# Second feed-forward layer in units of 512 tokens instead of 384, with four output accumulators

## Chip, cores and metric

One core of one Trainium2 chip. The metric is the device time of one execution in microseconds (us), median over several runs. The engines are TensorE (PE: matmuls, and PEld: its weight loads), VectorE (DVE), ScalarE (ACT), GpSimd (POOL) and SyncE (SP, which issues DMAs).

## What is computed

```python
y = linear_attention(q, k, v, alpha)              # batch 4, heads 8, 768 tokens, 48 channels
x = y.transpose(0, 2, 1, 3).reshape(3072, 384)
h = x @ w_in1                                     # 384 -> 2048
g = where(h >= 1, h, where(h <= -1, 0, (h + 1) ** 2 / 4))
x = g @ w_out1                                    # 2048 -> 384
h = x @ w_in2                                     # 384 -> 2048
out = (h * cos(h)) @ w_out2                       # 2048 -> 384
```

The weights come as float64; everything else is float32.

## The kernel before

The 3072 tokens are cut into NU = 8 units of N = 384. Attention comes first, chunk by chunk; the first layer runs beside it and after it, then the second layer. The 2048 hidden channels of a layer are FT = 16 hidden tiles of 128.

**Order of the program.** Every operation is handed to a list scheduler (`Order.add`) with its engine, a rough length, the operations it comes after and the ring buffers it takes (`buf(tag)`). The scheduler simulates the engines with these rough lengths and writes the instructions in the order in which they start there. Each engine then runs its own instructions strictly in that order on the chip. What a hidden tile of a unit needs is a *step*.

**Products.** A product of two float32 matrices is done as three matmuls on parts hi and lo (`mm3`): hi·hi + hi·lo + lo·hi. A step of the second layer (`step2(i)`, i = 16·unit + hidden tile) has 9 *input products* (`ff_in`: 3 blocks of model channels × 3 passes, 384 moving columns, the tokens, into one PSUM bank of h, h, sc, y by turns) and 9 *output products* (`ff_out`: 3 blocks of 128 tokens × 3 passes, 384 moving columns, the model channels, onto three accumulators). The accumulators of a unit are three of acc0, acc1, acc2, kv, one further with each unit; each collects 16 steps.

**Between input and output products** a step passes through a chain: ACT scales h into an angle (L1044), DVE rounds it to whole turns (`nearest`, L1048), subtracts (`rest`, L1051), ACT takes the sine (L1054), DVE multiplies by h (`product`, L1057), ACT rounds that to gh (L896), POOL computes gl = g − gh (L901). In PE's order the output products of step i stand behind the input products of step i + 2.

**Weights of the second layer.** Each of the 32 weight tiles (16 of w_in2, 16 of w_out2) needs two conversions of half a tile each, thus 64, on DVE: a shift (L343), a select of sign and exponent (L347) and a merge with the low word (L353), the last from a stage in `w_raw` or in the attention's buffers `am`; ACT and POOL make hi and lo of it (L364, L368). They are spread over the end of the first layer and the first steps of the second. The first layer's steps have two DVE instructions each (L947, L951).

**Once per unit** the inputs are split into x2s (ACT L1023, POOL L1027, three each), and the finished accumulators are copied out (`put`, two on ACT, one on DVE) and stored.

Of the kernel before, what the change touches and what calls it, by code (L numbers as in the profile page):

```python
# [45 lines left out]
class Buf:  # L46
    """A buffer of a ring: its first user takes a slot, its last one gives it back."""
# [16 lines left out]
class Order:  # L64
    """List scheduling: the operations of the program, each with its engine, a rough length in us,
    the operations it comes after and the buffers it takes, put into the order of emission."""
# [24 lines left out]
    def run(self):  # L91
# [10 lines left out]
        def since(op):  # L102
            """When op can start, or None."""
# [50 lines left out]
def gla_two_mlps(  # L154
# [60 lines left out]
    rings.update({f"{t}_2": 1 for t in SECOND})  # L215
    o = Order(rings, loose=("kv", "acc0", "acc1", "h"))
# [5 lines left out]
    # rough lengths in us  # L222
# [17 lines left out]
    # constants  # L240
# [7 lines left out]
    # buffers whose padding is written once  # L248
    am_b = [one.tile([P, 2, N], F32, name=f"am{i}") for i in range(2)]
    v_b = [one.tile([P, CH, 112], F32, name=f"v{i}") for i in range(NV)]  # L250
    raw_b = [one.tile([P, R * D], F32, name=f"raw{i}") for i in range(NRAW)]
# [29 lines left out]
    def weight(layer, kind, f, after=()):  # L281
        """One hidden tile; of the first layer's input weights, two come in one load."""
# [15 lines left out]
        if joint:  # L298
            pair_of["buf"] = rb

# [89 lines left out]
    SQUARES = []  # L390
    xraw = []
# [6 lines left out]
    def early_buffers():  # L398
        """The first unit's alpha, k and q have room where later units' x1 come."""
# [23 lines left out]
    def attention(m):  # L423
# [8 lines left out]
        def room(pool_, tag):  # L432
            if alt and tag in SECOND:
                return xraw[2][1][0][:, SECOND.index(tag), :]
            return pool_.tile([P, N], F32, tag=tag, name=tag)

        # loads
        loads, rawb = [], []
        for x, src in enumerate((alpha, k, q)):
# [31 lines left out]
            rawb.append(rb)  # L471
        if early:
            vb, v_ops = v0b, v0_ops
        else:
            vb = buf("v")

# [14 lines left out]
        # channel-major alpha, k, q; the running products F, then 1/F from the chunk's end  # L491
        ab, kb, qb, fb, gb, feb, amb = (
            buf(t + "_2" if alt and t in SECOND else t) for t in ("ta", "tk", "tq", "F", "G", "fe", "am")
        )
        if alt:
# [3 lines left out]
        def turn(x, pool_, tag, tb):  # L499
            def fn():  # L500
                d[tag] = room(pool_, tag)
# [17 lines left out]
        def evict(bank, tag, pool_, tb, after):  # L519
            def fn():  # L520
                d[tag] = room(pool_, tag)
# [4 lines left out]
        if turned:  # L526
            a_src, k_src, q_src = (buf("h") for _ in range(3))
            ta, tk, tq = (turn_by_pe(x, bank) for x, bank in enumerate((a_src, k_src, q_src)))
            if not k_direct:
                tk = evict(k_src, "tk", p2, kb, tk)  # L530
            if not q_direct:
                tq = evict(q_src, "tq", p2, qb, tq)
        else:
            a_src = ab
            ta, tk = turn(0, p1, "ta", ab), turn(1, p2, "tk", kb)
# [4 lines left out]
        def forward():  # L540
            d["F"] = room(p1, "F")
# [23 lines left out]
        if not turned:  # L565
            tq = turn(2, p2, "tq", qb)

        def last():
            d["G"] = room(p1, "G")
# [17 lines left out]
        def times(tag, src, by, direct, pool_, tb, by_buf, after):  # L587
            """k/F and q*F, from PSUM or in place."""
            def fn():
                if direct:  # L590
                    d[tag] = room(pool_, tag)
# [10 lines left out]
        ksc = times("tk", k_src if turned else kb, "G", k_direct, p2, kb, gb, [bw, tk])  # L602
        qs = times("tq", q_src if turned else qb, "F", q_direct, p2, qb, fb, [fw, tq])

        def square(i, nm):
            def fn():
                if turned and i == 0:
                    d["ta"] = room(p1, "ta")
# [13 lines left out]
        # k/F with the tokens on the partitions  # L622
# [39 lines left out]
        # products within the chunks: both heads at once, on the two halves of the array's rows  # L662
# [33 lines left out]
        # the state: what each chunk adds, then chunk by chunk  # L696
# [19 lines left out]
        def within_and_before(cs):  # L716
            """Outputs of the chunks cs: tokens of the same chunk, then the state before it."""
# [71 lines left out]
        # hi and lo parts; channels of the last two heads fill the gaps of the others' tiles  # L789
# [79 lines left out]
    def ff_in(layer, f, x, x_ops, xbuf, tag):  # L869
# [3 lines left out]
        def fn():  # L873
            h.tile = ps(tag)
            for j in range(KT):
                xt = x()
                mm3(
                    h.tile[:, 0:N],
# [7 lines left out]
            "pe", 3 * KT * pe(N), fn, [w_op, *x_ops, prev.get("in")], new=[h], use=[hb, lb, xbuf], span=6 * KT * pe(N) + STEP  # L886
# [4 lines left out]
    def split_g(g, rb, after, final=False):  # L891
        ghb, glb = buf("gh"), buf("gl")

        def high():
            ghb.tile = p3.tile([P, N], F32R, tag="gh", name="gh")
            nc.scalar.copy(ghb.tile, g())  # L896

        def low():
            glb.tile = p3.tile([P, N], F32R, tag="gl", name="gl")
# [3 lines left out]
        a = add("act", act(N, 0.04), high, [after], new=[ghb], use=[rb])  # L903
        a = add("dve" if final else "pool", dve(N) if final else pool(N), low, [a], new=[glb], use=[rb, ghb])
        return a, ghb, glb

    def ff_out(layer, f, acc, first, last, g):
# [3 lines left out]
        for c in range(KT):  # L911
# [25 lines left out]
    def step1(u, f, first, last, add_):  # L937
        h_op, h = ff_in(1, f, lambda: X1[u]["x"], X1OPS[u], X1B[u][0], "h")
        rb = buf("r")

        def relu():
            rb.tile = p3.tile([P, N], F32, tag="r", name="r")
# [10 lines left out]
        def below():  # L953
            rb.tile = p3.tile([P, N], F32, tag="r", name="r")
# [8 lines left out]
        if u < len(ACT_STEPS) and f in ACT_STEPS[u]:  # L963
            # min(r, 1) = 1 - relu(1 - r), and its square against h
# [48 lines left out]
    X2S = {}  # L1013

    def split_x2(u, after):
        t = {}
        xb = buf("x")
        ops = []
        for c in range(KT):
            def high(c=c):  # L1020
                if c == 0:
                    t["x"] = xp.tile([P, KT, 2, N], F32R, tag="x", name="x2s")
                nc.scalar.copy(t["x"][:, c, 0, :], X2[u // 2]["x"][:, u % 2, c, :])  # L1023

            def low(c=c):
                hi, lo = t["x"][:, c, 0, :], t["x"][:, c, 1, :]
                nc.gpsimd.tensor_tensor(out=lo, in0=X2[u // 2]["x"][:, u % 2, c, :], in1=hi, op=ALU.subtract)  # L1027
# [295 lines left out]
```

## Time and profile before

| | |
|---|---|
| median of 3 runs | 1039.32 us (1036.25 to 1042.29) |
| span of the profiled execution | 1041.0 us |
| PE busy | 976.2 us, 94% |
| DVE busy | 737.8 us, 71% |
| ACT, POOL busy | 487.1 us, 442.7 us |

The profiled execution is 1.7 us above the median. The second layer takes the stretch from about 602 us, when the first layer's last step leaves DVE, to 1033 us; its weights are still being converted until about 652 us. In the trace's views, a timeline row is "start in us, duration in us, engine, line, operation, output<-input, shapes, count", then in brackets how long the engine had been idle and what released it. A row of a group is "line, engine, operation, names, shapes, count | busy us, mean ns of one | idle time of the engine just before them, and by what it ended". A row of a window is "from:to, length, busy us (and count) of PE, PEld, DVE, ACT and POOL, granted clock of PE, DMA share, GB/s". Matmuls are pipelined, so one lasts longer than the distance from its start to the next one's; that distance is what it costs.

### The profile page before, as it was taken

The numbers are of one execution on the slowest core, as the hardware profiler recorded it, in microseconds if no ns is written. First come the engines' busy times: TensorE is split into PE (matmuls) and PEld (weight loads), VectorE is DVE, ScalarE is ACT, GpSimd is POOL, SyncE is SP. The second block draws the span as 40 slices with busy tenths as digits, with TensorE's granted clock in tenths as the row PEclk, the third lists the DMA queues.
The fourth block names the chain that finished last, engine by engine and source line by source line (L and its number), as shares of the span: only waits on it lengthen the run. The fifth ranks groups of instructions, "written<-read, shape, count | busy, mean of one in ns | idle before, by whom it ended". The sixth has DMA issues, their size and how long they took to land.

```text
span 1041.0 us, 17456 instructions
## 1 busy us (share of the span) xinstructions
PE 976.2 (94%) x6186; PEld 894.3 (86%) x6186; DVE 737.8 (71%) x1370; ACT 487.1 (47%) x1108; POOL 442.7 (43%) x458
## 2 busy tenths in 40 slices
PE   7998878999999999999999878999999999999996
PEld 6677867788888889889899777899999999999996
DVE  6899999876778767674448999656565656565653
ACT  4566555443333434433345565545454545454443
POOL 3266665443333333332246566434343434343332
PEclk9899999999999999999999989999999999999999
DMA  7968753443534334330203421000000000000000
GB/s 167 181 148 168 159 151 87 110 113 72 114 86 110 76 79 102 66 70 8 82 30 102 126 91 61 24 1 23 1 21 4 23 1 24 1 23 1 25 1 26
DMA packets 113553, 71.82 MB, mean 69 GB/s; under 512 B 71729, under 2 KB 96305, under 8 KB 113457
## 3 DMA queue, kind: packets, MB, share of 16 engines
q1 hardware_dynamic: 113456, 70.62, 28.5%
q8 instruction: 50, 0.82, 0.3%
q14 instruction: 47, 0.38, 0.1%
HBM read 58.79 MB, written 9.44 MB: 66 GB/s over the span
## 4 chain that ended last, share of the span: by engine, by line
DVE 28%; PE 11%; ACT 10%; issue 7%; POOL 1%; DVEq 0%; POOLq 0%; ACTq 0%
DVE turn L1048 8%; DVE ang L1051 7%; DVE ang L1057 6%; ACT ang L1054 6%; PE acc L865 5%; PE h L865 4%; ACT ang L1044 3%; DVE wz L353 2%; DVE wz L347 2%; DVE wz L343 1%; DVE h L947 0%; POOL gl L901 0%; PE y L865 0%; DVE r L951 0%; PE y L725 0%
## 5 line engine op out<-in xcount | busy, mean ns | idle before, releaser
L901 POOL TENSOR_TENSOR gl<-ang,gh 128x384 fp32r<-128x384 f32 x127 | 136.3, 1073 | 241.3 <-ACT gh L896 215.7
L901 POOL TENSOR_TENSOR gl<-r,gh 128x384 fp32r<-128x384 f32 x128 | 135.5, 1059 | 191.0 <-ACT gh L896 159.6
L865 PE MATMUL h<-x,winhi 128*128 128x384 f32 x768 | 201.9, 344 | 13.2 <-DVE r L951 8.1
L865 PEld LDWEIGHTS h<-x,winhi 128*128 128x128 f32 x768 | 140.2, 191 | 18.1 <-DVE r L951 10.8
L1048 DVE TENSOR_SCALAR turn<-ang 128x384 int32<-128x384 f32 x128 | 95.1, 743 | 72.6 <-ACT ang L1044 72.6
L865 PE MATMUL acc<-gh,wouthi 128*128 128x384 f32 x384 | 136.2, 355 | 3.7 <-DVE x L997 1.5
L1054 ACT ACTIVATE ang<-ang 128x384 f32<-128x384 f32 x128 | 67.3, 526 | 151.5 <-DVE ang L1051 151.5
L865 PE MATMUL acc<-gl,wouthi 128*128 128x384 f32 x384 | 131.7, 343 | 5.9 <-POOL gl L901 5.9
L865 PE MATMUL h<-x,winlo 128*128 128x384 f32 x384 | 131.0, 341 | 0.0
L865 PE MATMUL acc<-gh,woutlo 128*128 128x384 f32 x384 | 129.7, 338 | 0.0
L947 DVE TENSOR_TENSOR h<-r,h 128x384 f32<-128x384 f32 x119 | 66.3, 557 | 82.8 <-ACT r L943 82.8
L896 ACT CAST gh<-r 128x384 fp32r<-128x384 f32 x128 | 65.5, 511 | 101.0 <-DVE r L951 96.8
L865 PE MATMUL acc<-wouthi,gl 128*128 128x384 f32 x288 | 101.3, 352 | 8.7 <-POOL gl L901 8.7
L865 PE MATMUL acc<-wouthi,gh 128*128 128x384 f32 x288 | 98.8, 343 | 7.0 <-ACT x L999 2.4
L943 ACT ACTIVATE r<-h,half 128x384 f32<-128x384 f32 x119 | 68.8, 578 | 77.6 <-PE h L865 77.5
L865 PE MATMUL h<-x2s,winhi 128*128 128x384 f32 x384 | 97.7, 335 | 1.7 <-DVE r L951 1.7
L865 PE MATMUL acc<-woutlo,gh 128*128 128x384 f32 x288 | 97.6, 339 | 0.0
L896 ACT CAST gh<-ang 128x384 fp32r<-128x384 f32 x128 | 65.6, 513 | 55.3 <-DVE ang L1057 55.2
L1051 DVE TENSOR_TENSOR ang<-ang,turn 128x384 f32<-128x384 f32 x128 | 81.9, 640 | 11.7
L865 PEld LDWEIGHTS acc<-gh,wouthi 128*128 128x128 f32 x384 | 72.4, 189 | 12.3 <-issue 2.8
L865 PEld LDWEIGHTS acc<-gl,wouthi 128*128 128x128 f32 x384 | 72.5, 189 | 10.6 <-POOL gl L901 10.3
L865 PEld LDWEIGHTS h<-x,winlo 128*128 128x128 f32 x384 | 73.0, 190 | 0.2 <-POOL winlo L368 0.2
(152 smaller groups left out, 2109.0 us busy)
## 6 DMA issues: line engine op xcount, KB each, us to landing
w_raw<-in_moe_w_out_dram SPq DMA_DIRECT2D x18, 384.0 KB, 3.6
scr<-G SPq DMA_DIRECT2D x96, 48.0 KB, 1.8
ks<-scr SPq DMA_DIRECT2D x24, 192.0 KB, 2.8
out_dram<-o SPq DMA_DIRECT2D x24, 192.0 KB, 2.0
v<-in_v_dram SPq DMA_DIRECT2D x56, 72.0 KB, 2.4
w_raw<-in_moe_w_in_dram SPq DMA_DIRECT2D x10, 384.0 KB, 3.2
raw<-in_alpha_dram SPq DMA_DIRECT2D x48, 72.0 KB, 2.0
raw<-in_k_dram SPq DMA_DIRECT2D x48, 72.0 KB, 2.0
```

Source lines behind the costliest of these rows:

```text
L347: nc.vector.scalar_tensor_tensor(out=z, in0=t["y"], scalar=-(2**31), in1=z, op0=ALU.bitwise_and, op1=ALU.bitwise_or)
L353: nc.vector.scalar_tensor_tensor(out=z, in0=bits(0).bitcast(U32), scalar=29, in1=z, op0=ALU.logical_shift_right, op1=ALU.bitwise_or,)
L865: nc.tensor.matmul(o, lhsT=lhs[a], rhs=rhs[b], start=first and i == 0, stop=last and i == 2)
L896: nc.scalar.copy(ghb.tile, g())
L901: eng.tensor_tensor(out=glb.tile, in0=g(), in1=ghb.tile, op=ALU.subtract)
L943: nc.scalar.activation(rb.tile, h.tile[:, 0:N], AF.Relu, bias=half, scale=0.5)
L947: nc.vector.tensor_tensor(out=hh, in0=rb.tile, in1=hh, op=ALU.max)
L1044: nc.scalar.activation(rb.tile, h.tile[:, 0:N], AF.Copy, bias=0.25, scale=1.0 / TWO_PI)
L1048: nc.vector.tensor_scalar(out=tb.tile, in0=rb.tile, scalar1=1.0, scalar2=None, op0=ALU.mult)
L1051: nc.vector.tensor_tensor(out=rb.tile, in0=rb.tile, in1=tb.tile, op=ALU.subtract)
L1054: nc.scalar.activation(rb.tile, rb.tile, AF.Sin, scale=SIN_SCALE)
L1057: nc.vector.tensor_tensor(out=rb.tile, in0=rb.tile, in1=h.tile[:, 0:N], op=ALU.mult)
```

## The change

The second layer's units become M = 512 tokens, NU2 = 6 of them instead of 8: 96 steps instead of 128. An input product has 512 moving columns instead of 384, and so has every instruction of the chain; a step has 12 output products instead of 9 (four blocks of 128 tokens, 384 columns each) onto all four accumulators, and a unit ends with four copies out (two on ACT, two on DVE). The number of moving columns in all is the same: 128 × 18 × 384 = 96 × (9 × 512 + 12 × 384) = 884,736; the matmuls of the layer are 2016 instead of 2304.

The larger buffers lie in rooms that the attention and the first layer have left: angles in the rooms of the first layer's r and gh (4 buffers), turns in that of gl (2), the second layer's gh and gl in two tiles of x1 (4 each), the units' x2s by turns in `rv` (the attention's raw and v) and `amt` (am, tk, tq), the copies out in those of F, G, ta and ks. `over(...)` makes the first user of a room wait for the last ones of the old buffers.

```diff
+    rings.update({"xs": 2, "ang": 4, "turn": 2, "gh2": 4, "gl2": 4, "o0": 1, "o1": 1, "o2": 1, "o3": 2})
...
-    am_b = [one.tile([P, 2, N], F32, name=f"am{i}") for i in range(2)]
...
+    amt = one.tile([P, 8, N], F32, tag="amt", name="amt")
+    am_b = [amt[:, 2 * i:2 * i + 2] for i in range(2)]
...
+    rv = one.tile([P, NRAW * R * D + NV * CH * 112], F32, tag="rv", name="rv")
...
+    M = 512
+    NU2 = NT // M
+    G2 = M // P
...
+    def second_buffers():
+        def take_angles():
+            F2["ang"] = [t_[:, i] for tag in ("r", "gh") for t_ in [p1.tile([P, 2, M], F32, tag=tag, name="ang")] for i in range(2)]
+            t_ = p1.tile([P, 2, M], I32, tag="gl", name="turn")
+            F2["turn"] = [t_[:, i] for i in range(2)]
+
+        F2["op"] = add(None, 0.0, take_angles, over("r", "g"), lat=0.0)
...
     def step2(i):
-        u, f = divmod(i, FT)
-        t, xb, x_ops = X2S[u]
-        h_op, h = ff_in(2, f, lambda: t["x"], x_ops, xb, H2TAGS[i % len(H2TAGS)])
-        rb, tb = buf("r"), buf("ks")
+        u2, f = divmod(i, FT)
+        t, xb, x_ops = X2S[u2]
+        h_op, h = ff_in(2, f, lambda: t["x"], x_ops, xb, H2TAGS[i % len(H2TAGS)], M)
+        rb, tb = buf("ang"), buf("turn")
...
         if f == 0:
-            step2.acc = [buf(ACC2TAGS[(u * KT + c) % 4]) for c in range(KT)]
+            step2.acc = [buf(tag) for tag in ACC2TAGS]
...
-        for c in range(KT):
-            tag, pool_ = (("tk", p2), ("tk", p2), ("tq", p2))[c]
-            ob = buf(tag)
+        for c in range(G2):
+            ob = buf(f"o{c}")
...
-                copy = nc.vector.tensor_copy if c == 1 else nc.scalar.copy
+                copy = nc.vector.tensor_copy if c % 2 else nc.scalar.copy
```

Up to about 530 us of the trace of before the program's order is the same on all engines. The first place where the order matters below is DVE where the first layer ends. Here L951 is the last of the first layer's products, L343, L347 and L353 are the three instructions of a conversion (wy and wz its work buffers), and L1048, L1051 and L1057 are turn, rest and product of the second layer's first step. Before:

```order
L951 SCALAR_TENSOR_TENSOR r<-r,h 128x384
L347 SCALAR_TENSOR_TENSOR wz<-wy,wz 128x384
L353 SCALAR_TENSOR_TENSOR wz<-am_94,wz 128x384
L1048 TENSOR_SCALAR turn<-ang 128x384
L343 TENSOR_SCALAR wz<-wy 128x384
L1051 TENSOR_TENSOR ang<-ang,turn 128x384
L347 SCALAR_TENSOR_TENSOR wz<-wy,wz 128x384
L353 SCALAR_TENSOR_TENSOR wz<-w_raw,wz 128x384
L1057 TENSOR_TENSOR ang<-ang,h 128x384
```

After (where L973 is the first layer's last product, L353, L357 and L363 the conversion, L1109, L1112 and L1118 turn, rest and product, and L1019 a copy of a finished accumulator of the first layer):

```order
L973 SCALAR_TENSOR_TENSOR r<-r,h 128x384
L353 TENSOR_SCALAR wz<-wy 128x384
L357 SCALAR_TENSOR_TENSOR wz<-wy,wz 128x384 x2
L363 SCALAR_TENSOR_TENSOR wz<-w_raw,wz 128x384 x2
L353 TENSOR_SCALAR wz<-wy 128x384
L357 SCALAR_TENSOR_TENSOR wz<-wy,wz 128x384
L1019 COPY x_6030<-acc_6071 128x384
L353 TENSOR_SCALAR wz<-wy 128x384
L363 SCALAR_TENSOR_TENSOR wz<-w_raw,wz 128x384
L1109 TENSOR_SCALAR turn<-ang 128x512
L357 SCALAR_TENSOR_TENSOR wz<-wy,wz 128x384
L1112 TENSOR_TENSOR ang<-ang,turn 128x512
```

The first layer's last product now stands ahead of more of the conversions: 47 of the 64 are ahead of it instead of 51, and 4 stand between it and the second layer's first product instead of 2.

The second place is DVE where the last of the 64 conversions ends. Before:

```order
L343 TENSOR_SCALAR wz<-wy 128x384
L1057 TENSOR_TENSOR ang<-ang,h 128x384
L347 SCALAR_TENSOR_TENSOR wz<-wy,wz 128x384
L1048 TENSOR_SCALAR turn<-ang 128x384
L353 SCALAR_TENSOR_TENSOR wz<-w_raw,wz 128x384
L1051 TENSOR_TENSOR ang<-ang,turn 128x384
L1048 TENSOR_SCALAR turn<-ang 128x384
L1051 TENSOR_TENSOR ang<-ang,turn 128x384
L1057 TENSOR_TENSOR ang<-ang,sc 128x384
```

After:

```order
L363 SCALAR_TENSOR_TENSOR wz<-w_raw,wz 128x384
L1112 TENSOR_TENSOR ang<-ang,turn 128x512
L353 TENSOR_SCALAR wz<-wy 128x384
L357 SCALAR_TENSOR_TENSOR wz<-wy,wz 128x384
L1118 TENSOR_TENSOR ang<-ang,y 128x512
L363 SCALAR_TENSOR_TENSOR wz<-w_raw,wz 128x384
L1109 TENSOR_SCALAR turn<-ang 128x512
L1112 TENSOR_TENSOR ang<-ang,turn 128x512
L1118 TENSOR_TENSOR ang<-ang,h 128x512
```

The last conversion stood behind the tenth of the second layer's products and now stands behind the twelfth.

## Rows read from the trace of the kernel before

**Rows 1.** The page: the span.

```profile
span 1041.0 us, 17456 instructions
```

**Rows 2.** Windows: end of layer 1, rest of conversion, and what follows.

```profile
556.00:602.00 46.00, 39.60 (x210) 35.66 (x209) 44.88 (x66) 26.20 (x55) 29.50 (x28) 1.00 0.42 129
602.00:656.00 54.00, 42.18 (x212) 38.09 (x210) 50.83 (x77) 31.49 (x67) 31.92 (x28) 0.94 0.21 66
660.00:1020.00 360.00, 356.52 (x2013) 349.00 (x2012) 215.54 (x344) 171.05 (x367) 137.84 (x130) 1.00 0.04 12
```

**Rows 3.** Groups on DVE from 556 to 655 us.

```profile
L347 DVE SCALAR_TENSOR_TENSOR wz<-wy,wz 128x384 int32<-128x384 int32 x27 | 26.1, 967 | 0.3
L353 DVE SCALAR_TENSOR_TENSOR wz<-w_raw,wz 128x384 uint32<-128x384 uint32 x17 | 17.1, 1016 | 0.2
L343 DVE TENSOR_SCALAR wz<-wy 128x384 int32<-128x384 int32 x27 | 14.5, 537 | 0.6 <-POOL woutlo L368 0.6
L353 DVE SCALAR_TENSOR_TENSOR wz<-am,wz 128x384 uint32<-128x384 uint32 x10 | 9.6, 960 | 0.1
L1051 DVE TENSOR_TENSOR ang<-ang,turn 128x384 f32<-128x384 f32 x12 | 9.5, 795 | 0.1
L1048 DVE TENSOR_SCALAR turn<-ang 128x384 int32<-128x384 f32 x12 | 7.7, 638 | 1.3 <-ACT ang L1044 1.3
...
L1057 DVE TENSOR_TENSOR ang<-ang,h 128x384 f32<-128x384 f32 x6 | 3.3, 542 | 0.0
```

**Rows 4.** Timeline of DVE: last first-layer product, two turns, twelfth second-layer product.

```profile
602.08 0.54 DVE L951 SCALAR_TENSOR_TENSOR r<-r,h 128x384 f32<-128x384 f32 x1
...
604.67 0.35 DVE L1048 TENSOR_SCALAR turn<-ang 128x384 int32<-128x384 f32 x1
...
610.27 1.16 DVE L1048 TENSOR_SCALAR turn<-ang 128x384 int32<-128x384 f32 x1
...
654.67 0.55 DVE L1057 TENSOR_TENSOR ang<-ang,y 128x384 f32<-128x384 f32 x1
```

**Rows 5.** Timeline of POOL, beside the second of these turns.

```profile
609.89 1.32 POOL L901 TENSOR_TENSOR gl<-ang,gh 128x384 fp32r<-128x384 f32 x1
```

**Rows 6.** Timeline of PE: outputs of the eleventh step of layer 2.

```profile
655.14 0.44 PE L865 MATMUL acc<-wouthi,gh 128*128 128x384 f32 x1 [0.70 <-ACT gh L896]
```

**Rows 7.** Timeline of PE: first input, first output, next first input product.

```profile
627.15 0.51 PE L865 MATMUL sc<-x2s,winhi 128*128 128x384 f32 x2
...
628.71 0.34 PE L865 MATMUL acc<-wouthi,gh 128*128 128x384 f32 x1
...
630.30 0.51 PE L865 MATMUL y<-x2s,winhi 128*128 128x384 f32 x2
```

**Rows 8.** Window: a short stretch of layer 2's first steps.

```profile
614.77:617.95 3.18, 3.18 (x11) 3.18 (x11) 3.15 (x6) 1.97 (x4) 2.03 (x2) 0.50 0.44 134
```

**Rows 9.** Timeline of PE within that stretch.

```profile
616.04 0.84 PE L865 MATMUL y<-x2s,winhi 128*128 128x384 f32 x2
...
617.00 0.84 PE L865 MATMUL y<-x2s,winhi 128*128 128x384 f32 x2
```

**Rows 10.** Timeline of PE in the attention: small products, weights of 128 columns.

```profile
31.34 0.45 PE L630 MATMUL acc<-ident,tk 112*128 112x112 f32 x3
31.63 0.45 PE L630 MATMUL kv<-ident,tk 112*128 112x112 f32 x3
```

**Rows 11.** Timeline of PE: waits of two unit changes, four units apart.

```profile
729.77 0.44 PE L865 MATMUL acc<-wouthi,gl 128*128 128x384 f32 x1 [0.63 <-POOL gl L901]
...
937.44 0.45 PE L865 MATMUL acc<-wouthi,gl 128*128 128x384 f32 x1 [0.63 <-POOL gl L901]
```

**Rows 12.** Timeline of PE: the end.

```profile
1026.80 0.34 PE L865 MATMUL acc<-wouthi,gh 128*128 128x384 f32 x1
...
1030.27 0.45 PE L865 MATMUL acc<-wouthi,gl 128*128 128x384 f32 x1 [0.64 <-POOL gl L901]
...
1033.02 0.34 PE L865 MATMUL kv<-wouthi,gl 128*128 128x384 f32 x1
```

More of the change, by code (lines that the diff above doesn't have):

```diff
@@ L299, in weight @@
             pair_of["buf"] = rb
+        if layer == 2 and i > 2:
+            ARENAS["amt"].append(rb)
         def place():
@@ L471, in attention @@
             rawb.append(rb)
+            if not in_x:
+                ARENAS["rv"].append(rb)
         if early:
@@ L585, in attention, with times @@
         bw = add("dve", CH * 0.26, backward, [la], use=[a_src, feb, gb])
[L587 removed]
+        def times(tag, src, by, direct, tb, by_buf, after):
             def fn():
                 if direct:
[L591 removed]
+                    d[tag] = room(tag, tb)
                 eng = nc.vector if direct else nc.gpsimd
@@ L910, in ff_out @@
         ops = []
-        for c in range(KT):
+        for c in range(len(acc)):
             def fn(c=c):
@@ L1011, in step1, with over, take @@
             X2OPS[u, c] = [p]
-    X2S = {}
-    def split_x2(u, after):
+    M = 512
+    NU2 = NT // M
+    G2 = M // P
+    X2S, GX, F2 = {}, [], {}
+    def over(*names):
+        return [x for name in names for b_ in ARENAS[name] for x in b_.ops()]
+    def second_buffers():
[4 more added lines that the diff above has]
+        F2["op"] = add(None, 0.0, take_angles, over("r", "g"), lat=0.0)
+        for _ in range(2):
+            xb, t_ = buf("x"), {}
+            def take(t_=t_):
+                t_[0] = xp.tile([P, 4, M], F32R, tag="x", name="g2")
+            add(None, 0.0, take, new=[xb], lat=0.0)
+            GX.append((xb, t_))
@@ L1016, in split_x2 @@
+    def split_x2(u2):
         t = {}
-        xb = buf("x")
+        xb = buf("xs")
         ops = []
-        for c in range(KT):
[L1020 to L1027, printed above, removed]
-            a = add("act", act(N, 0.04), high, X2OPS[u, c] + after, new=[xb] if c == 0 else [], use=[xb] if c else [])
-            ops.append(add("pool", pool(N), low, [a], use=[xb]))
@@ L1031, in split_x2, with take, src, high @@
-        X2S[u] = (t, xb, ops)
+        def take():
+            tag = ("rv", "amt")[u2 % 2]
+            t["x"] = one.tile([P, KT, 2, M], F32R, tag=tag, name="x2s")
+        first = add(None, 0.0, take, over(("rv", "amt")[u2]) if u2 < 2 else [], new=[xb], lat=0.0)
+        parts, s0 = [], u2 * M
+        while s0 < (u2 + 1) * M:
+            e0 = min((s0 // N + 1) * N, (u2 + 1) * M)
+            parts.append((s0 // N, s0 % N, e0 - s0, s0 - u2 * M))
+            s0 = e0
+        for c in range(KT):
+            for u, at, n, to in parts:
+                def src(c=c, u=u, at=at, n=n):
+                    return X2[u // 2]["x"][:, u % 2, c, at:at + n]
+                def high(c=c, n=n, to=to, src=src):
+                    nc.scalar.copy(t["x"][:, c, 0, to:to + n], src())
+                def low(c=c, n=n, to=to, src=src):
+                    nc.gpsimd.tensor_tensor(
+                        out=t["x"][:, c, 1, to:to + n], in0=src(), in1=t["x"][:, c, 0, to:to + n], op=ALU.subtract
+                    )
+                a = add("act", act(n, 0.04), high, [*X2OPS[u, c], first], use=[xb, X2B[u // 2]])
+                ops.append(add("pool", pool(n), low, [a], use=[xb, X2B[u // 2]]))
@@ L1056, in product @@
         def product():
[L1057 to L1064 removed]
+            nc.vector.tensor_tensor(out=rb.tile, in0=rb.tile, in1=h.tile, op=ALU.mult)
+        a = add("act", act(M), angle, [h_op, F2["op"]], new=[rb], use=[h])
+        a = add("dve", dve(M / 2), nearest, [a], new=[tb], use=[rb])
+        a = add("dve", dve(M), rest, [a], use=[rb, tb])
+        a = add("act", act(M, 0.04), sine, [a, RELU[-1]], use=[rb])
+        a = add("dve", dve(M), product, [a], use=[rb, h])
+        g = split_g(lambda: rb.tile, rb, a, layer=2, final=i == NU2 * FT - 1)
         if f == 0:
[L1066 removed]
+            step2.acc = [buf(tag) for tag in ACC2TAGS]
         acc = step2.acc
@@ L1127, in gla_two_mlps @@
         weight(2, "out", f, after=GLA_END[-1:])
-    for u in range(NU):
-        split_x2(u, [])
+    second_buffers()
+    for u2 in range(NU2):
+        split_x2(u2)
         for f in range(FT):
-            step2(u * FT + f)
+            step2(u2 * FT + f)
     with tc.manual_schedule():
```

97 lines of the change are left out of this document (54 added, 43 removed).

## The prediction, made before the changed kernel ran

> **What bounds the kernel now.** I read the windows first, since the page's mean over the span [rows 1] hides stages. The second layer falls in two. From 556 to 656 us DVE is busy 44.88 of 46 and 50.83 of 54 us, PE only 39.60 and 42.18: DVE, which converts the weights, sets the pace. From 660 to 1020 us PE is busy 356.52 of 360 us and DVE 215.54: PE sets it [rows 2]. So a change is worth what it does to DVE's work up to the last conversion, and behind that what it does to PE's products and waits.
>
> I mark the border at one event: DVE has done all 64 conversions and twelve products of the chain, at 655.22 us [rows 4]. At the same moment PE starts the outputs of the layer's eleventh step, at 655.14 us, after waiting 0.70 us for gh [rows 6]. By then it has done 13 steps' input and 10 steps' output products, so 115 and 118 are left.
>
> **Prices of before.** Nine input products take 628.71 − 627.15 = 1.56 us, nine output products 630.30 − 628.71 = 1.59 us [rows 7]: 173.5 and 176.7 ns each. At the 2.4 GHz of that stretch (granted clock 1.00 [rows 2]) 384 columns are 160 ns, so 13.5 and 16.7 ns stand over. What is left costs 115 × 1.56 + 118 × 1.59 = 367 us. PE ends at 1033.02 + 0.34 = 1033.4 us [rows 12], 378.2 us after 655.14; so 11 us go to waits. Seven of them are visible: once per unit PE waits for gl. The waits at 729.77 and 937.44 us [rows 11] are four units apart, so a unit takes 51.92 us, against 16 × 3.15 = 50.4 of products: 1.5 us lost per unit. After PE's end come 7.6 us of copy, store and end.
>
> **A. The weight phase.** DVE's work up to the border is 27 conversions in rows 556 to 655 us, (26.1 + 17.1 + 14.5 + 9.6) / 27 = 2.49 us each, first-layer products, and twelve times turn, rest and product, 0.638 + 0.795 + 0.542 = 1.98 us [rows 3]. The change moves conversions behind the last first-layer product and a few places ahead of chain instructions, but the sum up to the border (64 conversions, twelve products) holds the same instructions. Only the twelve chains grow, by a third: 12 × 1.98 / 3 = +7.9 us, if DVE stays as full. So the border comes at about 662.8 us. PE then stands further: by the order of its instructions it has done 14 input and 11 output steps, of 512 tokens each, and 82 and 85 are left. At proportional prices these are 82 × 1.56 × 4/3 + 85 × 1.59 × 4/3 = 170.6 + 180.2 = 351 us, against 367: −16. With the +7.9 that is about −8. New is a wait for rooms: the first angle needs the first layer's last r and gh to be gone, and behind this ACT instruction the sine and the gh of the step queue, for which DVE and PE wait. PE runs four input steps ahead there, and DVE has four conversions between the last first-layer product and the first chain's product (two before), about 10 us of cover at 2.49 each. I allow 1.5 us; without that cover it would cost the length of one chain, some 5 us. **A = −7** (−9 to −2: the upper end is rival 2).
>
> **B. A product of 512 columns.** No row has one. The upper bound is proportional, 173.5 × 4/3 = 231 ns, and the lower its own columns, 512 / 2.4 = 213.3 ns. For a fixed rest of 13.5 ns speaks that the rest looks fixed per product. For the lower bound speaks the stretch with granted clock 0.50, which is 1.2 GHz [rows 8]: there three products take 617.00 − 616.04 = 0.96 us [rows 9], 320 ns each, which is 384 / 1.2 with nothing over. So the rest could be a floor under a product that longer ones don't feel. But a floor set by loading the weights would have to be about 173 ns, and in the attention three products of 112 columns, each with a weight of 128 columns of its own, follow in 31.63 − 31.34 = 0.29 us [rows 10], so 97 ns are enough there. I take 213.3 + 13.5 = 226.8 ns. **B** = 82 × 9 × (226.8 − 231.3) = **−3.3** (0 to −13). Output products keep 384 columns and their price.
>
> For a product behind another the Trainium skill (TensorE: Matmul & The Clock Gate, § Back-to-back issue gap) states columns / 2.4 + 2.5 ns for an isolated one. That is 162.5 ns at 384 columns, where the trace has 173.5 and so disagrees; at 512 it would be 215.8 ns, and B −10 by it.
>
> **C. Waits behind the border.** Between the end of a step's input products and its first output product lie two steps of PE: 2 × 3.15 = 6.3 us before, 2 × (9 × 226.8 + 12 × 176.7 ns) = 8.3 us after. The chain needs about 5.0 us: in the tail the last input products start at 1026.80 − 1.56 = 1025.24, where those of the step before end, and that step's gl is there at 1030.27 [rows 12]. A third more is 6.7 us. So the slack grows from 1.3 to 1.6 us, and there are five unit changes behind the first instead of seven. At a change three instructions on ACT and DVE (copies of the accumulators) push into the chain; four of them do it after, and all four accumulators must be free when the next unit's first outputs come, two steps' work later than acc0's last product but only one input step (2.0 us) after the fourth's. Two ACT and two DVE copies fit there. With 1.5 us lost per change as before, five changes instead of seven save 3 us; with the wider slack taking half of the rest it is 6. **C = −5** (0 to −7).
>
> **D. Tail.** The last step's chain and outputs are a third longer, behind waits of half a us [rows 12]: **+0.8**.
>
> **Sum:** −7 − 3.3 − 5 + 0.8 = −14.5 against the span of 1041.0, so 1026.5. The execution of the profile lies 1.7 us over the median, so 1024.8, rounded to **1024 us**.
>
> **Rivals.**
> *1. A product costs its own columns only* (rows 8 and 9 speak for it, rows 10 against a floor): 738 products × 13.5 ns = 10 us less, **1014**. Chance 0.12.
> *2. DVE's longer instructions collide with longer ones of POOL.* A turn takes 0.35 us alone and 1.16 us where a POOL instruction of 1.32 us runs [rows 4, 5]. Before the border some 17 conversions and chains meet a POOL instruction that is now a third longer, 0.35 to 0.4 us each: 6 to 7 us, **1031**. For it speaks that the mean turn in this stretch is 0.638 us, nearly twice the least; against it, that fewer, longer instructions meet as often in total. Chance 0.14.
> The Trainium skill (SBUF — State Buffer, § Who interferes with whom) says of DVE's instructions with two SBUF inputs, and of those in two-port modes, that they and GpSimd shut each other out for a whole instruction. By that rule rest and select wait as a turn does, and the trace agrees with 1.16 against 0.35 us.
> *3. The change does not do it*: price proportional (B = 0), waits per change as long as the slack allows (C = 0), A at −2: about −1, **1038**. For it speaks that moving columns are equal in number before and after. Chance 0.11.
> *4. Slower: the chain no longer fits.* It decides when the 512-column chain is longer than 8.3 us; from there every step behind the border waits, 82 times. At 8.6 us, if queues on ACT and POOL add nearly two more instructions of some 1 us to the 6.7 us, that is 0.3 × 82 = 25 us on the forecast, **1049**; up to 8.4 us the rest of the sum still covers it. Against it: the chain would have to grow from 5.0 us by 70% for a third more columns. Chance 0.07.
>
> **Chances.** Forecast 0.56, rivals 0.12, 0.14, 0.11, 0.07. A measurement of this kernel can tell 0.5% (5.2 us) from no change. Faster: forecast and rivals 1 and 2, 0.82; same 0.11; slower 0.07. The range 1013 to 1034 reaches from rival 1 past rival 2 and leaves out rivals 3 and 4, 0.18.
>
> **What the profile after should show.** The last first-layer product on DVE earlier than 602 us, by up to four conversions, 592 to 598. The twelfth product of the chain and the last conversion near 663 us, with DVE as full as before up to there. Products of 512 columns 227 ns apart (213 for rival 1, 231 for rival 3). Waits for gl at the unit changes shorter than 0.63 us. PE's end near 1018 us. The prediction is wrong if DVE idles for several us at the change of layers, if PE's clock falls behind the border, or if PE waits in every step.

## The result, and the profile after

The changed kernel takes 1047.58 us (median of 5 runs, 1045.34 to 1049.24) against 1039.32 us before: the ratio is 1.0071, with a 95% interval of 1.0047 to 1.0095. It is 0.7% slower where 1.5% faster was forecast, and outside the range. The profiled execution is, at 1045.34 us, the fastest of the five; its span of 1043.6 us lies 4.0 us below their median, while the span of before, 1041.0 us, lies 1.7 us above its median. So the two profiles differ by 2.6 us where the medians differ by 8.3. What follows compares the profiles.

Windows of the changed kernel over the stretches of [rows 2]:

```profile
556.00:602.00 46.00, 43.78 (x232) 40.24 (x231) 41.16 (x66) 27.27 (x55) 27.97 (x26) 1.00 0.37 121
602.00:656.00 54.00, 45.40 (x218) 38.56 (x218) 49.75 (x70) 31.01 (x61) 34.27 (x29) 0.99 0.19 59
660.00:1020.00 360.00, 351.94 (x1678) 297.44 (x1677) 210.41 (x250) 150.17 (x273) 123.78 (x103) 1.00 0.03 12
```

Up to 656 us the change gains: PE is busier in both stretches, DVE a little less. From 660 to 1020 us PE is busy 351.94 of 360 us; that looks like hardly a loss. But a matmul's recorded duration runs over the start of the next one, and covers a stall as long as this overlap. The count shows it: 1678 matmuls, 21 to a step, are 79.9 steps, which need 333 us at the 4.17 us of products per step worked out below. So 27 of the 360 us are lost. (The weight loads' 297.44 us can't be held against the 349.00 of before, since there are a sixth fewer of them.) What the idle time waits for from 684 to 1000 us is seen on the weight loads (the last columns are the idle time before them and what ended it), and hardly on PE's own waits (us in all, times, longest):

```profile
L882 PEld LDWEIGHTS acc<-wouthi,g 128*128 128x128 f32 x418 | 72.8, 188 | 28.7 <-POOL g L921 22.7 <-DVE o L1139 1.6 <-ACT o L1139 0.8
```

```profile
PE acc L882 <- POOL g L921: 2.5, 3, 1.1
```

PE's own waits show 2.5 us for POOL's gl (here called g, L921), its weight loads 22.7 us. The timeline of PE in one step shows where:

```profile
686.40 0.33 PE L882 MATMUL acc<-wouthi,g 128*128 128x384 f32 x1
...
695.36 0.33 PE L882 MATMUL acc<-wouthi,g 128*128 128x384 f32 x1
695.53 0.34 PE L882 MATMUL acc<-woutlo,g 128*128 128x384 f32 x1
695.90 0.61 PE L882 MATMUL acc<-wouthi,g 128*128 128x384 f32 x2
696.35 0.34 PE L882 MATMUL acc<-woutlo,g 128*128 128x384 f32 x1
...
697.74 0.63 PE L882 MATMUL y<-x2s,winhi 128*128 128x512 f32 x2
...
699.82 0.33 PE L882 MATMUL acc<-wouthi,g 128*128 128x384 f32 x1
...
702.21 0.39 PE L882 MATMUL h<-x2s,winhi 128*128 128x512 f32 x1
```

Nine input products of 512 columns take 699.82 − 697.74 = 2.08 us, 231 ns each. The step from 697.74 to 702.21 takes 4.47 us. Twelve output products at 174 ns (695.36 to 695.53 and most others) would be 2.09 us, so the step should take 4.17. Of the 0.30 us, 0.20 are lost in front of the third output product, the first that needs gl (695.90 − 695.53 = 0.37 instead of 0.17), and 0.10 in the two from there (696.35 − 695.90 = 0.45 instead of 0.35). Of the 74 steps from 684.3 to 1019.0 us, 57 come some 4.47 us apart like this one. Ten come at PE's own pace, 4.19 us; seven of these follow a stop of 2.2 us at 967 to 969 us, in which the chain could get ahead. The other seven lie at unit changes and take longer. What PE is waiting for is seen on the three engines of the chain, timelines of ACT, DVE and POOL of the changed kernel:

```profile
689.33 0.62 ACT L916 CAST g<-ang 128x512 fp32r<-128x512 f32 x1 [0.76 <-DVE ang L1118]
689.85 0.59 ACT L1105 ACTIVATE ang<-h 128x512 f32<-128x512 f32 x1
692.42 0.63 ACT L1115 ACTIVATE ang<-ang 128x512 f32<-128x512 f32 x1 [1.97 <-DVE ang L1112]
693.80 0.62 ACT L916 CAST g<-ang 128x512 fp32r<-128x512 f32 x1 [0.75 <-DVE ang L1118]
```

```profile
690.48 1.18 DVE L1109 TENSOR_SCALAR turn<-ang 128x512 int32<-128x512 f32 x1 [1.18 <-ACT ang L1105]
691.69 0.69 DVE L1112 TENSOR_TENSOR ang<-ang,turn 128x512 f32<-128x512 f32 x1
693.08 0.69 DVE L1118 TENSOR_TENSOR ang<-ang,h 128x512 f32<-128x512 f32 x1 [0.70 <-ACT ang L1115]
```

```profile
690.08 1.29 POOL L921 TENSOR_TENSOR g<-ang,g 128x512 fp32r<-128x512 f32 x1 [3.19 <-ACT g L916]
694.55 1.29 POOL L921 TENSOR_TENSOR g<-ang,g 128x512 fp32r<-128x512 f32 x1 [3.18 <-ACT g L916]
```

Read in order of time this is a ring: rounding to gh of one step (689.33, ACT), angle of the next step (689.85, ACT), turn (690.48), rest (691.69), sine (692.42, ACT), product (693.08), and then that step's gh (693.80, ACT), 4.47 us after the first. Every member starts when the one before ends; ACT and DVE both idle in between. On ACT the angle of the next step stands behind the gh of this one, though its h has been ready for some 3.4 us: the input products of the angle at 689.85 end where the output products at 686.40 begin. The chain itself, from that angle to the end of its gl at 695.84, takes 5.99 us; with the time in ACT's queue it is 9.4 us. So neighbouring chains overlap no further than this order allows, and a step takes one turn of this ring, whatever PE needs. In it the turn takes 1.18 us, most of it beside POOL's gl of the step before (690.08 to 691.37).

The end of the weight stretch, timelines of DVE and of PE (compare [rows 4, 6]), and PE's end:

```profile
586.84 0.54 DVE L973 SCALAR_TENSOR_TENSOR r<-r,h 128x384 f32<-128x384 f32 x1
...
651.03 0.68 DVE L1118 TENSOR_TENSOR ang<-ang,y 128x512 f32<-128x512 f32 x1
651.63 0.55 DVE L363 SCALAR_TENSOR_TENSOR wz<-w_raw,wz 128x384 uint32<-128x384 uint32 x1
```

```profile
652.42 0.44 PE L882 MATMUL acc<-wouthi,g 128*128 128x384 f32 x1 [1.90 <-ACT g L916]
...
1036.27 0.34 PE L882 MATMUL kv<-wouthi,g 128*128 128x384 f32 x1
```

The border (64 conversions, twelve products of the chain) comes at 652.2 us, with 14 input and 11 output steps done on PE, as forecast; PE goes on at 652.42. The first layer's last product stands at 586.84 us on DVE, earlier than the 592 to 598 us of the forecast.

### The profile page after: what moved, and what is told of

Its sections match the earlier page's. It is cut to its first block, busy times and chain, and to the rows that moved or that the text cites. A ratio compares the mean times of both kernels' runs of the same rounds, so it can differ in the third digit from the quotient of the medians.

```text
span 1043.6 us, 16458 instructions
## 1 busy us (share of the span) xinstructions
PE 977.8 (94%) x5898; PEld 845.2 (81%) x5898; DVE 737.1 (71%) x1278; ACT 471.0 (45%) x1020; POOL 436.4 (42%) x438
## 4 chain that ended last, share of the span: by engine, by line
DVE 28%; ACT 12%; PE 8%; issue 7%; POOL 1%; DMA 1%; SPq 0%; ACTq 0%; DVEq 0%
DVE turn L1109 10%; DVE ang L1112 7%; DVE ang L1118 6%; ACT ang L1115 5%; ACT ang L1105 5%; PE acc L882 4%; PE h L882 3%; DVE wz L353 2%; DVE wz L363 1%; DVE wz L357 1%; DMA w_raw<-in_moe_w_out_dram 1%; DVE h L969 1%; DVE r L973 0%; ACT wy L349 0%; PE y L742 0%
## 5 line engine op out<-in xcount | busy, mean ns | idle before, releaser
L921 POOL TENSOR_TENSOR g<-ang,g 128x512 fp32r<-128x512 f32 x95 | 124.6, 1312 | 256.7 <-ACT g L916 226.9
L921 POOL TENSOR_TENSOR gl<-r,gh 128x384 fp32r<-128x384 f32 x128 | 135.9, 1062 | 192.3 <-ACT gh L916 139.3
L882 PE MATMUL acc<-wouthi,g 128*128 128x384 f32 x576 | 173.5, 354 | 16.5 <-POOL g L921 9.5
L1109 DVE TENSOR_SCALAR turn<-ang 128x512 int32<-128x512 f32 x96 | 108.2, 1127 | 99.9 <-ACT ang L1105 99.9
L882 PEld LDWEIGHTS acc<-wouthi,g 128*128 128x128 f32 x576 | 101.4, 189 | 48.6 <-POOL g L921 34.4
L1115 ACT ACTIVATE ang<-ang 128x512 f32<-128x512 f32 x96 | 60.7, 632 | 170.9 <-DVE ang L1112 170.7
L882 PE MATMUL acc<-woutlo,g 128*128 128x384 f32 x288 | 97.3, 338 | 0.0
L882 PE MATMUL h<-x2s,winhi 128*128 128x512 f32 x288 | 89.7, 392 | 1.4 <-DVE ang L1118 1.4
L916 ACT CAST g<-ang 128x512 fp32r<-128x512 f32 x96 | 59.5, 620 | 64.1 <-DVE ang L1118 64.1
L1112 DVE TENSOR_TENSOR ang<-ang,turn 128x512 f32<-128x512 f32 x96 | 75.9, 791 | 2.8
L882 PEld LDWEIGHTS acc<-gh,woutlo 128*128 128x128 f32 x384 | 72.4, 189 | 0.0
```

What stands on the lines that cost most here:

```text
L882: nc.tensor.matmul(o, lhsT=lhs[a], rhs=rhs[b], start=first and i == 0, stop=last and i == 2)
L921: eng.tensor_tensor(out=glb.tile, in0=g(), in1=ghb.tile, op=ALU.subtract)
L1109: nc.vector.tensor_scalar(out=tb.tile, in0=rb.tile, scalar1=1.0, scalar2=None, op0=ALU.mult)
L1112: nc.vector.tensor_tensor(out=rb.tile, in0=rb.tile, in1=tb.tile, op=ALU.subtract)
L1115: nc.scalar.activation(rb.tile, rb.tile, AF.Sin, scale=SIN_SCALE)
```

## The experiments

Theory: **the serial ring** over ACT sets the step. Rival: **the chain is too long** for the two steps that lie between a step's input and output products, in whatever order its parts are queued. The trace above already speaks against the rival, since 5.99 us are less than those two steps; the runs try it. All runs below are on the changed kernel unless they say otherwise; the ratio in brackets is against the kernel before, run on the same chip, with its 95% interval. The kernel before had a median of 1036.32 us beside runs 1 to 4 and of 1039.23 us beside runs 5 to 8, so runs of the two groups are compared by their ratios as well.

**1. The next angle ahead of gh.** The only thing added is a dependency in the scheduler, from the angle of step i + 1 (`a`) to the rounding to gh of step i (`cast[0]`); the lines that keep `cast` are left out here. The scheduler then orders the rest by its own rules:

```diff
...
+        if cast and i > 0:
+            cast[0].after.append(a)
+            a.next.append(cast[0])
+            cast[0].need += 1
```

> The changed kernel with one thing moved: on ACT, the angle of step i+1 stands ahead of the rounding (gh) of step i. In the changed kernel's trace a steady step takes 4.475 us, the sum of gh, angle, turn, rest, sine and product one after the other, while PE's own products need 9 x 231.3 + 12 x 173.9 ns = 4.17 us. Theory 'serial loop' (ACT's order makes the chains of neighbouring steps follow each other without overlap): the loop falls to about 2.6 us, steps come every 4.17 to 4.2 us, PE's waits for gl in every step are gone, 75 steps x 0.3 us = 20 to 23 us less, span about 1021. Rival 'chain too long' (a 512-column chain needs more than the two steps of PE between input and output products, in whatever order): the chain is as long as before, so the step stays at 4.4 us or more and the time within 4 us of the changed kernel.

Measured: 1011.99 us (0.9755, 0.9726 to 0.9785), 35.6 us less than the changed kernel (33 by the ratios); the profile's span is 1010.8 us. The timeline of ACT in the steady stretch:

```profile
694.64 0.60 ACT L1107 ACTIVATE ang<-y 128x512 f32<-128x512 f32 x1 [1.73 <-PE y L882]
695.14 0.61 ACT L917 CAST g<-ang 128x512 fp32r<-128x512 f32 x1
696.46 0.63 ACT L1117 ACTIVATE ang<-ang 128x512 f32<-128x512 f32 x1 [0.71 <-DVE ang L1114]
698.83 0.60 ACT L1107 ACTIVATE ang<-h 128x512 f32<-128x512 f32 x1 [1.73 <-PE h L882]
```

The turn of the first of these angles on DVE, and its gl on POOL:

```profile
695.27 0.43 DVE L1111 TENSOR_SCALAR turn<-ang 128x512 int32<-128x512 f32 x1 [1.64 <-ACT ang L1107]
```

```profile
700.07 1.70 POOL L922 TENSOR_TENSOR g<-ang,g 128x512 fp32r<-128x512 f32 x1 [2.48 <-ACT g L917]
```

A window of the run:

```profile
684.00:1000.00 316.00, 315.38 (x1582) 285.08 (x1581) 146.66 (x236) 140.20 (x253) 141.60 (x94) 1.00 0.03 11
```

The same window of the changed kernel:

```profile
684.00:1000.00 316.00, 308.57 (x1468) 260.30 (x1467) 184.74 (x220) 130.38 (x236) 106.69 (x88) 1.00 0.03 11
```

The angle now waits for PE, not PE for the chain. A step takes 698.83 − 694.64 = 4.19 us, and 1582 instead of 1468 matmuls start in the same 316 us. The weight loads are busy 285.08 instead of 260.30 us. The rival "chain too long" is refuted: from the angle at 694.64 to the end of its gl at 701.77 the chain takes 7.1 us, longer than the 5.99 of the changed kernel, and PE doesn't wait for it. But the move does two things at once, for the turn now also begins ahead of POOL's gl and takes 0.43 us instead of 1.18 (the wait goes over to POOL, 1.70 us instead of 1.29). The gain is larger than the 20 to 23 us expected. Part of that is that PE gets through more of the weight stretch, 49.88 us busy from 602 to 656 us instead of 45.40, and part that no step from 684 to 1000 us takes longer than 4.68 us, at the unit changes neither.

**2. gl on DVE**, ACT's order untouched:

```diff
-            eng = nc.vector if final else nc.gpsimd
+            eng = nc.vector if final or layer == 2 else nc.gpsimd
```

> The changed kernel with gl computed on DVE instead of POOL, at the same places of the order, ACT's order untouched. Theory 'serial loop, closed by the turn's wait beside POOL': the turn falls from 1.17 to about 0.42 us since no POOL instruction runs beside it; gl (0.69 us on DVE) lies beside the next angle; loop about 3.75 us, under PE's 4.17, so 20 to 23 us less, span about 1021. Rival 'a turn of 512 columns simply lasts 1.17 us, the port has no part': the loop stays at 4.475 us or gets longer by what gl adds on DVE (up to 5.1 us), so 0 to 45 us more. In the stretch up to the last weight conversion DVE has 14 x 0.69 = 10 us more work, which may give back up to 10 us of the gain.

Measured: 1012.37 us (0.9776, 0.9747 to 0.9806). A turn in the timeline of DVE:

```profile
694.20 0.43 DVE L1109 TENSOR_SCALAR turn<-ang 128x512 int32<-128x512 f32 x1 [0.27 <-ACT ang L1105]
```

Without a POOL instruction beside it the same turn takes 0.43 us, not 1.18. With that the ring is 0.75 us shorter, 3.7 us, under PE's 4.17, and the steps come 4.19 us apart although ACT's order is still the serial one. So the serial order alone does not cost the 0.30 us; it does so together with the turn's wait beside POOL. (No run has the wait without the serial order, since run 1 removes both.) The Trainium skill (SBUF — State Buffer, § Who interferes with whom) gives the rule for that wait: a DVE instruction in a two-port mode, which `tensor_scalar` can enter, and one of GpSimd lock each other out, and whichever is issued first keeps the ports for its whole length. 1.18 against 0.43 us agrees with it. The prediction cited the rule for the weight stretch alone; here the wait decides the steady stretch.

**3. The turn straight from PSUM**: DVE computes it from h (times 1/2π, plus 0.25), so that it stands beside the angle and not behind it. It is also handed to the scheduler ahead of the angle, and the rest waits for both:

```diff
...
-            nc.vector.tensor_scalar(out=tb.tile, in0=rb.tile, scalar1=1.0, scalar2=None, op0=ALU.mult)
+            nc.vector.tensor_scalar(
+                out=tb.tile, in0=h.tile, scalar1=1.0 / TWO_PI, scalar2=0.25, op0=ALU.mult, op1=ALU.add
+            )
...
+        b = add("dve", dve(M), nearest, [h_op, F2["op"]], new=[tb], use=[h])
         a = add("act", act(M), angle, [h_op, F2["op"]], new=[rb], use=[h])
-        a = add("dve", dve(M / 2), nearest, [a], new=[tb], use=[rb])
-        a = add("dve", dve(M), rest, [a], use=[rb, tb])
+        a = add("dve", dve(M), rest, [a, b], use=[rb, tb])
```

> The changed kernel with the turn computed from h in PSUM (multiply by 1/2pi, add 0.25, round), so that it doesn't wait for the angle and reads no SBUF; ACT's order untouched (gh of a step ahead of the next angle). Theory 'serial loop': without the turn the loop is gh 0.53, angle 0.62, rest 0.72, sine 0.66, product 0.72 = 3.2 us, or up to 4.05 us if the rest (two SBUF inputs) now takes the wait beside POOL that the turn had; both lie under 4.17 us, so steps of 4.17 to 4.2 us and 18 to 23 us less, span 1021 to 1026. Rival 'chain too long': the chain loses about 1.2 us as well, so the rival too expects a gain here; this run and the first tell them apart only together (rival: gain here, none in the first).

Measured: 1021.57 us (0.9847, 0.9819 to 0.9874). Steps of 4.19 us again. ACT, timeline:

```profile
694.16 0.60 ACT L1105 ACTIVATE ang<-h 128x512 f32<-128x512 f32 x1 [0.77 <-DVE turn L1109]
```

The angle now starts only when the turn has ended, though it needs nothing of it: both read the same PSUM bank. The releasers in brackets come from semaphores, so it is the program that makes ACT wait here; what the chip would do without that is not shown. The ring closes with this wait in it and still fits. Why this run is 9 us slower than the first lies in front of the steady stretch (PE busy 43.19 us from 602 to 656 us, against 49.88); I did not take it further.

**4. The kernel before with the angle first**, the same edit as in the first run:

> The kernel before (384 tokens, three accumulators) with the same move on ACT: the angle of step i+1 ahead of gh of step i. There the same serial loop would be 3.7 us against PE's 3.15, but in its order about every second or third step already has the angle first. Theory 'serial loop': the waits for gl at the unit changes (1.5 us in each of seven) shrink, 3 to 9 us less, span 1032 to 1038; then the first run (512 tokens, same move) is faster than this one by 10 to 16 us, which is what units of 512 tokens are worth by themselves. Rival 'the waits at unit changes come from the copies out, not from this order': no change within 2 us.

Measured: 1040.49 us (1.0035, 1.0016 to 1.0054): no gain, a little slower. My expectation fell. The waits of PE from 684 to 1000 us (us in all, times, longest) are no longer for gl, but

```profile
PE acc L865 <- DVE o L1084: 4.3, 4, 1.1
PE kv L865 <- DVE o L1084: 1.1, 1, 1.1
```

waits for DVE's copy of an accumulator at unit changes, 5.4 us. The rival named there, that waits at unit changes have to do with the copies out, fits better. It also shows that at 384 columns the scheduler's own order, which lets the angle go first every third step, was good enough. The second part of the expectation failed too: run 1 is faster than this one by 28.5 us, where 10 to 16 were expected; why was not tried.

**5. The rough length of the turn.** One number, 0.34 us before:

```diff
-        a = add("dve", dve(M / 2), nearest, [a], new=[tb], use=[rb])
+        a = add("dve", 1.17, nearest, [a], new=[tb], use=[rb])
```

> The changed kernel with one number changed: the scheduler's rough length of the turn (nearest) is 1.17 us, as the changed kernel's trace has it in the steady stretch, instead of 0.34 us. The scheduler then puts the angle of a later step ahead of the rounding gh of an earlier one by itself. Theory 'the serial order of ACT comes from the rough length of the turn': steps of 4.17 to 4.2 us, 25 to 35 us less than the changed kernel, 1012 to 1022. Rival 'the length has no part in it, the order comes from the number of buffers': steps of 4.4 us and more, within 5 us of the changed kernel.

Measured: 1011.02 us (0.9732, 0.9692 to 0.9771). ACT's order of two neighbouring instructions, in the changed kernel:

```order
L916 CAST g_5983<-ang 128x512
L1105 ACTIVATE ang<-h 128x512
```

and with the turn's measured length:

```order
L1105 ACTIVATE ang<-h 128x512
L916 CAST g_5983<-ang 128x512
```

The scheduler puts the angle ahead of gh by itself once it counts with the turn's length beside POOL. The serial order came from that one number. In the order that follows the turn no longer meets gl and takes 0.43 us, as in run 1.

**6. The kernel before with gl on DVE**, the pair to the second run:

> The kernel before (384 tokens) with gl computed on DVE instead of POOL, at the same places of the order: the pair to the second run, so that the two sizes are compared without the serial loop and without the wait beside POOL. If 512 tokens are worth by themselves what the weight stretch gives (16 us of products less to do behind the border, twelve chains a third longer before it), this run lies at 1025 to 1032 and the second run is 13 to 20 us faster. Rival 'units of 512 are worth nothing once the loops are open': this run within 5 us of the second, 1008 to 1017.

Measured: 1026.38 us (0.9892, 0.9847 to 0.9938); the second run is 14.0 us faster, 12 by the ratios. In this pair, with gl on DVE at both sizes, units of 512 tokens are worth 1.2 to 1.4%, much as forecast. The other pair, runs 1 and 4, gives 28.5 us, so the figure hangs on the order of the rest. In this run PE's matmuls and its weight loads are both busy in the whole window, with no wait left to show:

```profile
684.00:1000.00 316.00, 316.00 (x1805) 315.53 (x1805) 200.12 (x409) 158.17 (x327) 16.67 (x15) 1.00 0.04 12
```

**7. Angle first and gl on DVE together:**

> Both moves of the first two runs together: the next angle ahead of gh on ACT, and gl on DVE. If after either one PE sets the steady steps alone (4.17 us of products, 4.19 measured), the second adds nothing there, and what is left to gain is the stretch up to the last weight conversion and the tail: 0 to 6 us less than the first run, 1006 to 1012. If instead the loop were still in the way, 10 us or more.

Measured: 1008.62 us (0.9705, 0.9664 to 0.9747), 3.4 us less than the first run (5 by the ratios), as expected for a ring that is already open.

**8. No angle.** The turn comes from PSUM as in the third run; the rest is h/2π − turn in one DVE instruction, and the quarter is a bias of the sine. The angle's instruction is gone:

```diff
...
-            nc.vector.tensor_tensor(out=rb.tile, in0=rb.tile, in1=tb.tile, op=ALU.subtract)
+            nc.vector.scalar_tensor_tensor(
+                out=rb.tile, in0=h.tile, scalar=1.0 / TWO_PI, in1=tb.tile, op0=ALU.mult, op1=ALU.subtract
+            )
...
-            nc.scalar.activation(rb.tile, rb.tile, AF.Sin, scale=SIN_SCALE)
+            nc.scalar.activation(rb.tile, rb.tile, AF.Sin, bias=quarter, scale=SIN_SCALE)
...
-        a = add("act", act(M), angle, [h_op, F2["op"]], new=[rb], use=[h])
...
```

> The changed kernel without the angle on ACT: DVE rounds h/2pi + 0.25 straight from PSUM, subtracts the turn from h/2pi in one instruction (h from PSUM, turn from SBUF), and the quarter comes as a bias of the sine. gl stays on POOL. Per step ACT loses 0.6 us, DVE has one instruction with PSUM as source in place of one from SBUF. The loop product, gh, ... no longer closes over ACT, and none of the chain's DVE instructions reads two operands from SBUF, so none should wait beside POOL: steady steps of 4.17 to 4.2 us, and a shorter chain in the weight stretch, 1003 to 1014. If the waits beside POOL have another cause than two SBUF operands, turn and rest last 1 us or more on the average there and the time is that of the third run, about 1021.

Measured: 1006.00 us (0.9689, 0.9653 to 0.9725), the lowest median of all, though not clear of run 7's; by the ratios it is 3.1% under the kernel before and 3.8% under the changed one. The groups of turn and rest from 684 to 1000 us:

```profile
L1113 DVE SCALAR_TENSOR_TENSOR ang<-h,turn 128x512 f32<-128x512 f32 x36 | 24.9, 691 | 3.6
L1107 DVE TENSOR_SCALAR turn<-h 128x512 int32<-128x512 f32 x36 | 24.9, 691 | 42.7 <-PE h L884 42.7
```

Both take 691 ns on the average, though gl is on POOL: nothing of the chain on DVE waits beside POOL any more.

## Why the prediction was wrong

PE's end was forecast at 1018.9 us (the sum less what follows it) and came at 1036.6: +17.7 us. The span came 17.1 us above the forecast 1026.5. The median came 22.8 us above the 1024.8 worked out from that, 5.7 us more, since the span of before lies above its median and that of after below; these 5.7 us are not explained here. Two of the prediction's signs of being wrong came: PE waits in most steps, and its clock falls behind the border. By the steps:

- **C, the waits behind the border: this step failed; with the tail, D, it is off by about 29 us.** From 652.42 to 1036.6 us are 384.2 us; the products that are left take 82 × 9 × 231.3 + 85 × 12 × 173.9 ns = 348.1 us. So 36.1 us were lost, where the working of C and D left 11 − 5 + 0.8 = 6.8. The 74 steps from 684.3 to 1019.0 us hold 26.3 us of it: 17.3 in the 57 steps of 4.47 us, 8.7 in the seven at unit changes, which the forecast saw getting cheaper. Another 4.8 us lie before 684.3 and 5.0 in the tail. The step compared one chain's length (6.7 us) with the lead of two steps (8.3 us) and found it fits. That is true of a chain alone (5.99 us), but the engines in it work on neighbouring steps in a fixed order, and the ring gh, angle, turn, rest, sine, product has to fit into *one* step: 4.47 us against 4.17. Runs 1 and 5 show it by ACT's order (with the turn's wait going as well), runs 2 and 3 by the turn alone.
- **Rival 4 had the sign and the symptom, not the mechanism.** It asked for a chain longer than 8.3 us, by waits in ACT's and POOL's queues, with PE waiting in every step. That is what a step shows, 9.4 us with 3.4 of them in ACT's queue. But the chain's instructions were never too long: they take 5.99 us, and 7.1 in run 1, where PE does not wait. It saw the queues as a length on top of the chain, not the ring that they close. Its 1049 us lies close to the measured 1047.58 by luck: its 25 us stand on a sum whose A was 12 us off. Its chance of 0.07 was too small.
- **A, the weight stretch: right in kind, mis-sized by 12 us.** PE's state at the border was as forecast (14 and 11 steps). The border was forecast at 664 us with the allowed idle time (662.8 there; 655.22 + 7.9 is 663.1, which changes little) and PE went on at 652.4. With the 351 us of products forecast for then, that is 1003.4, against 655.1 + 367.0 = 1022.1 before: A was −19, not −7. The twelve chains did become dearer, 1.030 + 0.920 + 0.679 = 2.63 us each instead of 1.98, +7.8 us, just the forecast 7.9. But a conversion, which I held at 2.49 us, took (17.1 + 16.2 + 11.0 + 7.7) / 25 = 2.08 (groups on DVE of the changed kernel from 556 to 652 us):

```profile
L353 DVE TENSOR_SCALAR wz<-wy 128x384 int32<-128x384 int32 x25 | 17.1, 692 | 3.0 <-POOL woutlo L378 2.3 <-POOL winlo L378 0.6
L357 DVE SCALAR_TENSOR_TENSOR wz<-wy,wz 128x384 int32<-128x384 int32 x25 | 16.2, 663 | 0.1
L1112 DVE TENSOR_TENSOR ang<-ang,turn 128x512 f32<-128x512 f32 x12 | 12.4, 1030 | 0.1
L1109 DVE TENSOR_SCALAR turn<-ang 128x512 int32<-128x512 f32 x12 | 11.0, 920 | 1.1 <-ACT ang L1105 1.1
L363 DVE SCALAR_TENSOR_TENSOR wz<-w_raw,wz 128x384 uint32<-128x384 uint32 x15 | 11.0, 748 | 0.0
L363 DVE SCALAR_TENSOR_TENSOR wz<-amt,wz 128x384 uint32<-128x384 uint32 x10 | 7.7, 781 | 0.0
...
L1118 DVE TENSOR_TENSOR ang<-ang,h 128x512 f32<-128x512 f32 x6 | 4.1, 679 | 0.4 <-ACT ang L1115 0.4
```

  That is 25 × 0.41 = 10 us, and DVE was two conversions and two first-layer steps further at 556 us. It idled more in return. In run 6, with gl off POOL, the same conversions cost less as well ([rows 3]: 967 for the select, there 852 ns), which suggests that their price hangs on what POOL runs beside them; whether the new order meets POOL less, and why, was not tried and stays open. Rival 2 feared the opposite.
- **B, the price of a product: the upper bound was right.** 231 ns, proportional to the columns, not 226.8: +3.3 us. Rival 1 and its 213 ns are refuted. The Trainium skill (TensorE: Matmul & The Clock Gate, § Back-to-back issue gap) states columns / 2.4 + 2.5 ns for an isolated product; its 215.8 ns are not in this trace either. (By 215.8 ns B would be 738 × (215.8 − 231.3) = −11 us, not the −10 of the prediction.) The output products went from 176.7 to 173.9 ns, −2.9 us.
- **D, the tail:** about 5 us, where 0.8 was added to what was there. Two waits on PE's timeline, and behind them products of 512 columns that are (1029.19 − 1028.34) / 2 = 0.43 us apart, 512 / 1.2, at half clock:

```profile
1024.71 0.45 PE L882 MATMUL acc<-wouthi,g 128*128 128x384 f32 x1 [1.04 <-ACT g L916]
1026.12 0.44 PE L882 MATMUL acc<-wouthi,g 128*128 128x384 f32 x1 [0.79 <-POOL g L921]
...
1028.34 1.05 PE L882 MATMUL y<-x2s,winhi 128*128 128x512 f32 x2
1029.19 0.63 PE L882 MATMUL y<-x2s,winlo 128*128 128x512 f32 x1
```

  The same happens behind the border, after waits of 1.90 and 1.20 us at 652.42 and 654.23. Windows of both stretches (the granted clock is the third number from the end):

```profile
655.40:658.40 3.00, 3.00 (x10) 2.71 (x9) 1.80 (x2) 1.11 (x2) 2.82 (x4) 0.50 0.00 0
1027.00:1030.50 3.50, 3.50 (x11) 2.88 (x10) 0.76 (x2) 1.83 (x3) 1.26 (x1) 0.52 0.00 0
```

  At half clock products take twice as long, so each stretch costs about 1.5 us (an estimate: half its length).

The sum of it: −12 (A) + 3.3 − 2.9 (B) + 29.3 (C and D) = +17.7 us. The forecast's own claim about the change, that 512 tokens are worth about 14.5 us, is near what runs 2 and 6 measure without the ring, 12 to 14 us. That is luck in part, since A was 12 us off, and the pair of runs 1 and 4 measures 28.5.

## What to carry to other kernels

Checking that one chain fits into the lead it is given is not enough: follow the ring from an instruction to the same instruction of the next step, along the data and along each engine's order, and compare it with what the bounding engine needs for *one* step. A kernel whose order is written by a scheduler with rough lengths has to have them measured again when sizes change; here one length of 0.34 instead of 1.17 us cost 35 us, more than twice what the change is worth by runs 2 and 6. And a busy share of PE near 98% can hide a wait in every step: look at the distance from start to start, or at what the weight loads wait for.

## What the runs showed of the hardware

A product of 512 columns takes 4/3 of one of 384 at full clock (231 and 173.5 ns), although at half clock 384 columns take 320 ns with nothing over. A turn (int32 from float32, SBUF to SBUF) of 512 columns takes 0.43 us alone and 1.18 us when a POOL subtraction of 1.29 us has begun before it; read from PSUM it takes 0.69 us beside POOL too (runs 3 and 8). Where the turn and the rest begin first, POOL's subtraction takes 1.70 us instead (run 1). And PE's granted clock fell to half in two stretches, 0.50 from 655.40 to 658.40 us behind waits of 1.90 and 1.20 us, and 0.52 from 1027.00 to 1030.50 us behind waits of 1.04 and 0.79 us.
